# Softmax sums in another order: other merged pairs of P tiles, a later sum, and a new start of the output projection

## The chip, the cores and the metric

The kernel runs on one core of a Trainium2 chip. The metric is the device time of one execution in microseconds (us). TensorE (PE) multiplies matrices, VectorE (DVE), ScalarE (ACT) and GpSimd (POOL) do the elementwise work, and SyncE (SP) issues most DMAs.

## The reference

Two layers alternate over x of 2048 tokens by 1024 features, float32. `_A` is full softmax attention with 32 heads of 32 features; `_B` scores every token and passes only the eight best through a feed-forward block.

```python
def _A_ref(x, wqkv, wo):
    qkv = (x @ wqkv).reshape(B, S, 3, H, Dh).transpose(2, 0, 3, 1, 4)
    q, k, v = qkv[0], qkv[1], qkv[2]
    p = softmax(einsum("bhqd,bhkd->bhqk", q, k) * Dh ** -0.5)
    o = einsum("bhqk,bhkd->bhqd", p, v)
    return o.transpose(0, 2, 1, 3).reshape(B, S, D) @ wo

def _B_ref(x, w_r, w_gate, w_up, w_down):
    r = x @ w_r
    idx = argsort(-r)[:, :8]
    x_sel = take_along_axis(x, idx)
    y = ((silu(x_sel @ w_gate) * (x_sel @ w_up)) @ w_down) * sigmoid(r_sel)
    return x + scatter_add(zeros, idx, y)

for _ in range(2):
    x = x + _A_ref(layernorm(x), wqkv, wo)
    x = x + _B_ref(layernorm(x), w_r, w_gate, w_up, w_down)
```

## The kernel before

`layer(n, ...)` runs twice. Every engine works through its own list in the order in which the code writes it; what overlaps follows from semaphores alone.

**Projections of q, k and v** (`proj`). 24 column blocks (b) of the weights are multiplied with each of four chunks (c) of 512 tokens. Weights are float32 cut into two parts: ACT casts the high part `wh` from the loaded `wraw` (L498), POOL subtracts for the low part `wl` (L499), and a product is three matmuls, `wh` with `xh`, `wl` with `xh`, `wh` with `xl` (L552 to L554). Results go to DRAM, from where the attention's q and k are loaded. In the last chunk, at b = 3, SP issues the loads of the first keys, and from b = 6 on `proj` slips the first row maxima of the scores in between (`pre_half`, matmuls L444, maxima L448), which need the keys' first slot. That slot holds the high and low parts (j = 0 and 1) of a head; j = 2 fills the second slot. ACT's cast of each block's result is L567.

**Attention.** 32 units (eight groups of four heads, four chunks of 512 queries) of 16 steps each. A step takes 128 keys (kt) for four heads: PE computes scores (L459), ACT exponentiates them into one of nine `P` tiles (L758), and in the next step PE multiplies P with v (L684). Row maxima for a unit 25 steps ahead are found beside it, four reductions on DVE per step (L452) of scores that PE makes for it alone (L444). A new P tile overwrites the one of nine steps earlier, so its exponent waits for the last reader of that one.

The softmax denominators need the sum of all 16 P tiles of a unit. Two of them (`DIRECT`, 14 and 15) are summed by PE straight away. Five pairs are merged by an accumulating DMA that POOL issues (`MERGED`: tile k + 1 added into tile k, L697, 1 MB each), and POOL adds what is left, eight adds a unit, into `acc` (`ADDED`, pairs of a step and a tile, L694). At step `SUM_AT`, counted from the unit's start and so lying in the next unit, PE sums `acc` and the direct tiles with a matrix of ones (`sum_mm`, L704). These lists set the order on POOL:

```python
ev = [(k + 2, "end", 0, "merge", (k, k + 1)) for k in MERGED]
ev += [(at, "end", 1, "add", (k, 0 if at == ADDED[0][0] else None, False)) for at, k in ADDED]
return ev + [(SUM_AT, "mid", 5, "sum", ())]
```

The last unit of a layer does its adds on DVE, and its steps carry no more maxima.

**Output projection.** For each of 16 tiles of 128 tokens the attention's result `oraw` is scaled by the reciprocal denominators `rden` (L807), cut into `oh` (ACT, L810) and `ol` (DVE, L811), and multiplied with `woh` and `wol`, the two parts of `wo`, in 48 matmuls into one of two `pre` tiles (L850 to L854). DVE adds the residual x (L856), takes the layernorm (L120, L869) and the router's score (L870, which also writes into the `pre` tile and so frees it). The last unit's result and sums go to DRAM, and the second half of the denominators (`xn` from `sd`) is read back and inverted on DVE (L729) before the loop over tiles starts. In the second layer POOL scatters each finished tile to the output (L875). The feed-forward block follows; in the first layer it runs beside the next layer's projections.

## Time and profile before

| | before |
|---|---|
| median of three runs | 4854.77 us (4845.85 to 4872.93) |
| the profiled execution | 4860.6 us, of which the span of the instructions is 4858.7 us |
| busy: PE, DVE, POOL, ACT | 95%, 67%, 66%, 50% of the span |
| mean granted TensorE clock | 0.976 |

All durations below are from the one profiled execution. PE is busy nearly all the time, but a matmul's end is modelled, and a busy share over the whole span hides which stage waits for what. The two attentions take up the larger part of the span: the exponents run from 614.0 to 4525.9 us, with the output projection, the feed-forward block and the second projections between the layers.

### The profile page before, as it was taken

Reading aid. Unit: us, or ns where it says so; the run is one execution under the profiler, and the core shown is the slowest. Engines: PE = TensorE matmul, PEld = TensorE weight load, DVE = VectorE, ACT = ScalarE, POOL = GpSimd, SP = SyncE. Lnnn points to the kernel's source line nnn. Section 1 sums busy time; section 2 is a strip of 40 time slices with the busy share of each in tenths; the row PEclk is TensorE's granted clock in tenths of the full one; section 3 lists DMA queues with packets and bytes.
Section 4 is the critical chain, followed back from the end, with each engine's and each line's share of the span. In section 5 each row is a group of like instructions: output and inputs, shape, how many; then the busy total and the mean of one; then the engine's idle time right before and its main releaser. Section 6 shows DMA issues by size and latency. Waiting matters only on the chain. (4 is left out here: it accounts for less than half of the span.)

```text
span 4858.7 us, 73884 instructions
## 1 busy us (share of the span) xinstructions
PE 4609.1 (95%) x29438; PEld 2702.2 (56%) x29438; DVE 3233.4 (67%) x4943; ACT 2422.7 (50%) x2550; POOL 3227.5 (66%) x1251
## 2 busy tenths in 40 slices
PE   8999999999999999979799999999999999999796
PEld 6887745444444454437577777544444444444472
DVE  3221578788888888866522225888888888886753
ACT  2222266666666666640122222766676666767200
POOL 4443368888888888944433432888888888888341
PEclk9999999999999999999899999999999999999897
DMA  6656467676777777749688664867777777767477
GB/s 196 186 174 176 134 152 162 145 167 141 172 146 157 158 154 154 164 103 257 216 241 266 195 178 126 172 143 163 155 163 154 156 152 159 169 143 161 130 226 295
DMA packets 341433, 833.10 MB, mean 171 GB/s; under 512 B 43296, under 2 KB 175392, under 8 KB 291152
## 3 DMA queue, kind: packets, MB, share of 16 engines
q0 software_dynamic: 47168, 333.63, 34.1%
q1 hardware_dynamic: 284512, 465.38, 32.9%
q10 hardware_dynamic: 9408, 29.37, 2.3%
q8 instruction: 231, 3.78, 0.3%
q14 instruction: 114, 0.93, 0.1%
HBM read 384.01 MB, written 119.18 MB: 104 GB/s over the span
## 5 line engine op out<-in xcount | busy, mean ns | idle before, releaser
L452 DVE TENSOR_REDUCE nm<-st 128x1 f32<-128x512 f32 x3896 | 2424.6, 684 | 443.2 <-PE st L444 431.6
L758 ACT ACTIVATE P<-pre 128x1024 f32<-128x1024 f32 x2048 | 1985.7, 1022 | 771.9 <-PE pre L459 459.5
L694 POOL TENSOR_TENSOR acc<-acc,P 128x2048 f32<-128x2048 f32 x434 | 1999.2, 4607 | 406.1 <-DMA P<-P 346.0
L459 PE MATMUL pre<-q,ks 64*128 64x512 f32 (+1 forms) x8192 | 1162.0, 400 | 8.3 <-ACT P L758 7.5
L684 PE MATMUL pv<-P,v 128*32 128x512 f32 x8192 | 1094.8, 607 | 3.0 <-DMA v<-vd 3.0
L444 PEld LDWEIGHTS st<-ks,q 64*128 64x128 f32 x3896 | 536.1, 185 | 911.3 <-DVE nm L452 766.1
L444 PE MATMUL st<-ks,q 64*128 64x512 f32 x3896 | 973.6, 471 | 0.4
L499 POOL TENSOR_TENSOR wl<-wraw,wh 128x2048 fp32r<-128x2048 f32 (+1 forms) x97 | 441.9, 4556 | 683.4 <-ACT wh L498 651.3
L459 PEld LDWEIGHTS pre<-q,ks 64*128 64x128 f32 (+1 forms) x8192 | 774.3, 188 | 211.3 <-ACT P L758 79.7
L552 PE MATMUL st<-xh,wh 128*128 128x512 f32 x1536 | 617.0, 402 | 2.2 <-ACT xh L525 2.2
L554 PE MATMUL st<-xl,wh 128*128 128x512 f32 x1536 | 601.9, 392 | 0.6 <-DVE xl L526 0.5
L553 PE MATMUL st<-xh,wl 128*128 128x512 f32 x1536 | 600.7, 391 | 0.0
L568 DVE TENSOR_TENSOR lo<-st,hi 128x512 fp32r<-128x512 f32 x128 | 88.2, 689 | 434.0 <-ACT hi L567 434.0
L567 ACT CAST hi<-st 128x512 fp32r<-128x512 f32 x128 | 75.3, 588 | 566.3 <-PE st L554 566.3
L552 PEld LDWEIGHTS st<-xh,wh 128*128 128x128 f32 x1536 | 289.9, 189 | 107.1 <-issue 33.4
L697 POOL DMA_DIRECT2D P<-P x310 | 294.0, 948 | 64.7 <-PE st L444 64.1
L554 PEld LDWEIGHTS st<-xl,wh 128*128 128x128 f32 x1536 | 289.5, 188 | 64.5 <-DVE xl L526 1.7
L553 PEld LDWEIGHTS st<-xh,wl 128*128 128x128 f32 x1536 | 290.1, 189 | 56.1
L684 PEld LDWEIGHTS pv<-P,v 128*32 128x32 f32 x8192 | 162.2, 108 | 267.9 <-issue 263.1
L694 POOL TENSOR_TENSOR acc<-P 128x2048 f32<-128x2048 f32 x62 | 301.9, 4869 | 0.0
L850 PE MATMUL pre<-woh,oh 128*128 128x512 f32 x512 | 208.4, 407 | 53.1 <-DVE pre L870 43.1
L535 DVE COPY vn<-st 128x512 f32<-128x512 f32 x64 | 44.3, 691 | 304.0 <-PE st L533 304.0
(163 smaller groups left out, 2555.5 us busy)
## 6 DMA issues: line engine op xcount, KB each, us to landing
P<-P POOLq DMA_DIRECT2D x310, 1024.0 KB, 8.5
wraw<-in_A_wqkv_dram SPq DMA_DIRECT2D x96, 1024.0 KB
q<-qh SPq DMA_DIRECT2D x256, 128.0 KB
ks<-kh SPq DMA_DIRECT2D x128, 256.0 KB
fw<-in_B_w_down_dram SPq DMA_DIRECT2D x28, 1024.0 KB
qh<-hi SPq DMA_DIRECT2D x64, 256.0 KB
ql<-lo SPq DMA_DIRECT2D x64, 256.0 KB
kh<-hi SPq DMA_DIRECT2D x64, 256.0 KB
```

What stands on the lines that cost most here:

```text
L444: pe.matmul(ps[b], Q[u][rows, i, 0, qt * 128:(qt + 1) * 128], KS[(u // QC) % 2][rows, i, 0, j * 512:(j + 1) * 512], start=True, stop=True, ...
L452: dve.tensor_reduce(NM[u][:, j, 2 * i + b:2 * i + b + 1, qt], ps[b], axis=AX.X, op=OP.max, negate=True)
L459: pe.matmul(p[:, b * 512:(b + 1) * 512], KS[(u // QC) % 2][rows, i, slot, kt * 128:(kt + 1) * 128], Q[u][rows, i, slot, :], start=(slot == ...
L499: pool.tensor_tensor(wl[:, :, sl], raw[:, :, sl], wh[:, :, sl].bitcast(F32), op=OP.subtract)
L552: pe.matmul(p, wh[:, a, wsl], xh[:, a, :], start=(a == 0), stop=False)
L553: pe.matmul(p, wl[:, a, wsl], xh[:, a, :], start=False, stop=False)
L554: pe.matmul(p, wh[:, a, wsl], xl[:, a, :], start=False, stop=(a == KD - 1))
L684: pe.matmul(PV[u][32 * h:32 * h + 32, :], V[g][:, kt, 32 * h:32 * h + 32], P[s][:, h, :], start=(kt == 0), stop=(kt == NT - 1), tile_posit ...
L694: (dve if on_dve else pool).tensor_tensor(o, a, P[u * NT + k].rearrange("p h c -> p (h c)"), op=OP.add)
L697: pool.dma_start(P[u * NT + a], P[u * NT + b], accum_op=OP.add)
L758: act.activation(P[s][:, 2 * i:2 * i + 2, :].rearrange("p h c -> p (h c)"), p, AF.Exp, scale=SCALE)
L850: pe.matmul(p[:, bl], oh[:, a, :], woh[:, a, bl], start=(a == 0), stop=False)
```

## The change

Four edits. The pairs to merge are now written with their step, `(2, 0)` merging tiles 0 and 1 at step 2; pairs, order and steps of POOL's adds are others, and the sum is one step later. In the projections the first maxima start at b = 7, and the keys are loaded j by j, so that the first slot of all heads comes first. At the start of the output projection all eight casts `woh` are ACT's and all eight subtractions `wol` are DVE's, alternating; the loads stand in another order, and both `oraw` tiles are scaled first. In the loop over tiles the reciprocal of the second half stands behind the first tile's residual add and the third tile's split, and PE's matmuls go block by block of `wo`, both halves of the output in each.

```diff
-MERGED = (2, 4, 6, 8, 11)
-ADDED = ((5, 1), (7, 2), (8, 4), (12, 6), (13, 8), (14, 10), (17, 11), (19, 13))
+MERGED = ((2, 0), (8, 6), (11, 8), (13, 10), (15, 12))
+ADDED = ((5, 3), (6, 0), (9, 5), (12, 4), (14, 6), (15, 8), (16, 10), (20, 12))
+FIRST = 2
-SUM_AT = 21
+SUM_AT = 22
-    ev = [(k + 2, "end", 0, "merge", (k, k + 1)) for k in MERGED]
-    ev += [(at, "end", 1, "add", (k, 0 if at == ADDED[0][0] else None, False)) for at, k in ADDED]
+    ev = [(at, "end", 0, "merge", (k, k + 1)) for at, k in MERGED]
+    ev += [(at, "end", 1, "add", (k, FIRST if at == ADDED[0][0] else None, False)) for at, k in ADDED]
...
-                proj(2 * wb + i, c, c == 3 and b >= 6)
+                proj(2 * wb + i, c, c == 3 and b >= 7)
...
-                        for h in range(4):
-                            for j in range(3):
+                        for j in range(3):
+                            for h in range(4):
                                 load_k(0, h, j)
...
-            load_o(0, sync)
-            load_o(1, sync)
-            load_x(0)
-            split_o(0)
             woh = wp.tile([128, KD, D], F32R, name="woh", bufs=1)
+            load_x(0)
+            wrb = wp.tile([128, D], F32, name="wrb", bufs=1)
+            load_o(0, sync)
+            load_o(1, sync)
+            for t in range(2):
+                scale_o(t)
+                OT[t] = tuple(wp.tile([128, NG, 128], F32R, name=i) for i in ("oh", "ol"))
...
-            for a in range(KD):
-                (act.copy, dve.tensor_copy)[a % 2](woh[:, a, :], WOR[:, a, :])
-            for a in range(KD):
-                (dve, pool)[a % 2].tensor_tensor(wol[:, a, :], WOR[:, a, :], woh[:, a, :].bitcast(F32), op=OP.subtract)
+            for a in range(KD):
+                act.copy(woh[:, a, :], WOR[:, a, :])
+                if a == 0:
+                    split_o(0)
+                dve.tensor_tensor(wol[:, a, :], WOR[:, a, :], woh[:, a, :].bitcast(F32), op=OP.subtract)
             split_o(1)
+            load_x(1)
             load_o(2)
             load_o(3)
+            dma(wrb, w_r[None, :].to_broadcast([128, D]))
...
             sum_load(second, 1)
-            recip(second, 1)
-            dma(wrb, w_r[None, :].to_broadcast([128, D]))
...
                 if t + 2 < NT:
                     split_o(t + 2)
+                if t == 0:
+                    recip(second, 1)
```

On POOL, in the attention's first unit before the change: the tiles of steps 2 to 10 are 4194, 4224, 4254, 4285, 4317, 4349, 4389, 4421 and 4451, those of 11 to 13 are 4482, 4512 and 4542; the last two rows belong to the next unit.

```order
L694 TENSOR_TENSOR acc_4314<-acc_4314,P_4194 128x2048
L697 DMA P_4317<-P_4349 128x2048
L694 TENSOR_TENSOR acc_4314<-acc_4314,P_4254 128x2048
L697 DMA P_4389<-P_4421 128x2048
L694 TENSOR_TENSOR acc_4314<-acc_4314,P_4317 128x2048
L697 DMA P_4482<-P_4512 128x2048
L694 TENSOR_TENSOR acc_4314<-acc_4314,P_4389 128x2048
L694 TENSOR_TENSOR acc_4314<-acc_4314,P_4451 128x2048
L694 TENSOR_TENSOR acc_4314<-acc_4314,P_4482 128x2048
L694 TENSOR_TENSOR acc_4314<-acc_4314,P_4542 128x2048
L697 DMA P_4697<-P_4727 128x2048
L694 TENSOR_TENSOR acc_4837<-P_4632,P_4665 128x2048
```

The same place after the change; here steps 4 to 13 are 4255, 4285, 4317, 4349, 4388, 4419, 4450, 4480, 4511 and 4541, and the next unit begins with 4632.

```order
L698 DMA P_4317<-P_4349 128x2048
L695 TENSOR_TENSOR acc_4314<-acc_4314,P_4285 128x2048
L698 DMA P_4388<-P_4419 128x2048
L695 TENSOR_TENSOR acc_4314<-acc_4314,P_4255 128x2048
L698 DMA P_4450<-P_4480 128x2048
L695 TENSOR_TENSOR acc_4314<-acc_4314,P_4317 128x2048
L698 DMA P_4511<-P_4541 128x2048
L695 TENSOR_TENSOR acc_4314<-acc_4314,P_4388 128x2048
L695 TENSOR_TENSOR acc_4314<-acc_4314,P_4450 128x2048
L698 DMA P_4632<-P_4666 128x2048
L695 TENSOR_TENSOR acc_4314<-acc_4314,P_4511 128x2048
L695 TENSOR_TENSOR acc_4818<-P_4697,P_4728 128x2048
```

Before, one add stands between the merge into 4317 and the add that reads it, and likewise for 4389; now two adds stand between each merge and its add.

On DVE, at the start of the first layer's output projection, before:

```order
L811 TENSOR_TENSOR ol<-oraw,oh 128x1024
L827 CAST woh<-wor 128x1024 x4
L829 TENSOR_TENSOR wol<-wor,woh 128x1024 x4
L807 TENSOR_TENSOR oraw<-oraw,rden 128x1024
L811 TENSOR_TENSOR ol<-oraw,oh 128x1024
L729 RECIPROCAL xn<-xn 64x512
L856 TENSOR_TENSOR x<-pre,x 128x1024
L807 TENSOR_TENSOR oraw<-oraw,rden 128x1024
L811 TENSOR_TENSOR ol<-oraw,oh 128x1024
L120 BN_STATS bst<-x 128x6 x2
```

And after:

```order
L807 TENSOR_TENSOR oraw<-oraw,rden 128x1024 x2
L816 TENSOR_TENSOR ol<-oraw,oh 128x1024
L836 TENSOR_TENSOR wol<-wor,woh 128x1024 x8
L816 TENSOR_TENSOR ol<-oraw,oh 128x1024
L863 TENSOR_TENSOR x<-pre,x 128x1024
L807 TENSOR_TENSOR oraw<-oraw,rden 128x1024
L816 TENSOR_TENSOR ol<-oraw,oh 128x1024
L730 RECIPROCAL xn<-xn 64x512
L121 BN_STATS bst<-x 128x6 x2
```

The four casts are gone from DVE, four subtractions are added, and the reciprocal has moved behind three operations of the first and third tile.

On SP, the loads of the first keys in the first layer's last chunk, after the change (before, the twelve `ks` rows go head by head, `kh`, `kl`, `kh` for each):

```order
L72 DMA ks0_126<-kh0_109 32x2048 x4
L72 DMA ks0_126<-kl0_110 32x2048 x4
L72 DMA ks0_126<-kh0_109 32x2048 x4
L72 DMA wraw_3213<-in_A_wqkv_dram 128x8x256
L72 DMA qh0_107<-hi_3240 128x512
```

The twelve loads are the same and the weight block `wraw_3213`, used from b = 8 on, still stands directly behind them; the eight of the first slot now come first, where the last of them was the eleventh.

## Rows read from the trace of the kernel before

**Rows 1.** Groups of instructions over the whole span: busy us, mean ns, idle before.

```profile
L452 DVE TENSOR_REDUCE nm<-st 128x1 f32<-128x512 f32 x3896 | 2424.6, 684 | 443.2 <-PE st L444 431.6
L694 POOL TENSOR_TENSOR acc<-acc,P 128x2048 f32<-128x2048 f32 x434 | 1999.2, 4607 | 406.1 <-DMA P<-P 346.0 <-PE st L444 24.8 <-PE pre L459 12.4
L758 ACT ACTIVATE P<-pre 128x1024 f32<-128x1024 f32 x2048 | 1985.7, 1022 | 771.9 <-PE pre L459 459.5 <-ACT P L758 156.9 <-POOL acc L694 115.8
...
L694 POOL TENSOR_TENSOR acc<-P 128x2048 f32<-128x2048 f32 x62 | 301.9, 4869 | 0.0
L697 POOL DMA_DIRECT2D P<-P x310 | 294.0, 948 | 64.7 <-PE st L444 64.1 <-ACT P L758 0.6
```

**Rows 2.** One line's instructions in three stretches (one copy a unit): count, first and last start.

```profile
L709 ACT COPY o<-pv x30: 591/592/593, 663.7 to 2048.0; 128x512 f32<-128x512 f32 x30
...
L709 ACT COPY o<-pv x30: 590/592/593, 3071.4 to 4441.7; 128x512 f32<-128x512 f32 x30
...
L709 ACT COPY o<-pv x5: 590/592/592, 3071.4 to 3254.7; 128x512 f32<-128x512 f32 x5
```

**Rows 3.** Timeline of DVE in one step: start, duration, [idle before <-who ended it].

```profile
1226.71 2.48 DVE L452 TENSOR_REDUCE nm<-st 128x1 f32<-128x512 f32 x4 [0.22 <-PE st L444]
```

**Rows 4.** Timeline of POOL within one unit.

```profile
1217.61 0.88 POOL L697 DMA_DIRECT2D P<-P  x1
1222.09 4.58 POOL L694 TENSOR_TENSOR acc<-acc,P 128x2048 f32<-128x2048 f32 x1 [3.60 <-DMA P<-P]
1226.62 0.87 POOL L697 DMA_DIRECT2D P<-P  x1
...
1231.94 1.01 POOL L697 DMA_DIRECT2D P<-P  x1
```

**Rows 5.** DMA issues of the page: count, KB each, median us to landing.

```profile
P<-P POOLq DMA_DIRECT2D x310, 1024.0 KB, 8.5
```

**Rows 6.** Adds (L694) in the second layer's last unit: stretch, DVE busy, POOL busy.

```profile
4485.40:4503.30 17.90, 17.58 (x3) 15.56 (x3) 0.88 0.06 16
4503.30:4527.60 24.30, 22.92 (x10) 0.00 (x0) 0.95 0.05 14
```

**Rows 7.** Timeline of ACT around b = 6 of the first layer's last chunk.

```profile
476.00 0.59 ACT L567 CAST hi<-st 128x512 fp32r<-128x512 f32 x1 [4.85 <-PE st L554]
492.28 1.91 ACT L498 CAST wh<-wraw 128x2048 fp32r<-128x2048 f32 x1 [15.69 <-DMA wraw<-in_A_wqkv_dram]
495.72 0.59 ACT L567 CAST hi<-st 128x512 fp32r<-128x512 f32 x1 [1.53 <-PE st L554]
502.95 0.59 ACT L567 CAST hi<-st 128x512 fp32r<-128x512 f32 x1 [6.64 <-PE st L554]
```

**Rows 8.** Timeline of POOL at the same place.

```profile
494.27 4.60 POOL L499 TENSOR_TENSOR wl<-wraw,wh 128x2048 fp32r<-128x2048 f32 x1 [22.06 <-ACT wh L498]
```

**Rows 9.** Stretch: PE, PEld, DVE, ACT, POOL busy, granted clock, DMA share, GB/s.

```profile
482.00:492.00 10.00, 4.29 (x9) 2.83 (x10) 1.87 (x2) 0.00 (x0) 0.00 (x0) 0.51 1.05 245
```

**Rows 10.** Timeline of DVE at the start of the second layer's output projection.

```profile
4531.90 1.23 DVE L807 TENSOR_TENSOR oraw<-oraw,rden 128x1024 f32<-128x1024 f32 x1 [4.32 <-DMA rden<-rd]
...
4542.15 9.00 DVE L829 TENSOR_TENSOR wol<-wor,woh 128x1024 fp32r<-128x1024 f32 x4
...
4553.40 1.23 DVE L811 TENSOR_TENSOR ol<-oraw,oh 128x1024 fp32r<-128x1024 f32 x1 [1.12 <-ACT oh L810]
4567.17 3.34 DVE L729 RECIPROCAL xn<-xn 64x512 f32<-64x512 f32 x1 [12.54 <-DMA xn<-sd]
...
4575.03 1.28 DVE L120 BATCH_NORM_STATS2 bst<-x 128x6 f32<-128x512 f32 x2
```

**Rows 11.** Timeline of PE: the third tile's first matmul there.

```profile
4579.78 0.77 PE L850 MATMUL pre<-woh,oh 128*128 128x512 f32 x1 [13.96 <-DVE pre L870]
```

**Rows 12.** One line's instructions, both layers: duration ns min/median/max.

```profile
L829 DVE TENSOR_TENSOR wol<-wor,woh x8: 1212/2304/3408, 2147.7 to 4549.9; 128x1024 fp32r<-128x1024 f32 x8
```

**Rows 13.** Timeline of SP at the start of the first layer's output projection.

```profile
2133.13 1.71 SPq L803 DMA_DIRECT2D rden<-rd  x4
```

More of the change, by code (lines that the diff above doesn't have):

```diff
@@ L803, in load_o, with scale_o @@
                     eng.dma_start(RD[t][32 * h:32 * h + 32], rd[t, h:h + 1].to_broadcast([32, NG, 128]))
+            def scale_o(t):
+                dve.tensor_tensor(OR[t], OR[t], RD.pop(t), op=OP.mult)
             def split_o(t):
+                if t not in OT:
+                    scale_o(t)
+                    OT[t] = tuple(wp.tile([128, NG, 128], F32R, name=i) for i in ("oh", "ol"))
                 raw = OR.pop(t)
-                dve.tensor_tensor(raw, raw, RD.pop(t), op=OP.mult)
-                oh = wp.tile([128, NG, 128], F32R, name="oh")
-                ol = wp.tile([128, NG, 128], F32R, name="ol")
+                oh, ol = OT[t]
                 act.copy(oh, raw)
                 dve.tensor_tensor(ol, raw, oh.bitcast(F32), op=OP.subtract)
-                OT[t] = (oh, ol)
             def load_x(t):
@@ L835, in layer @@
             store_sum(NU - 1, last_sum, rest[:, 512:1024])
-            second = wp.tile([128, D], F32, name="xn", bufs=1)[0:64, 0:512]
+            second = XN[0:64, 0:512]
             sum_load(second, 1)
-            recip(second, 1)
-            dma(wrb, w_r[None, :].to_broadcast([128, D]))
             wor.close()
@@ L847, in layer @@
                 halves = [slice(0, 512), slice(512, 1024)]
-                for bl in halves:
-                    for a in range(KD):
+                for a in range(KD):
+                    for bl in halves:
                         pe.matmul(p[:, bl], oh[:, a, :], woh[:, a, bl], start=(a == 0), stop=False)
                         pe.matmul(p[:, bl], ol[:, a, :], woh[:, a, bl], start=False, stop=False)
-                for bl in halves:
-                    for a in range(KD):
+                for a in range(KD):
+                    for bl in halves:
                         pe.matmul(p[:, bl], oh[:, a, :], wol[:, a, bl], start=False, stop=(a == KD - 1))
```

8 lines of the change are left out of this document (5 added, 3 removed).

## Prediction

> **What bounds the kernel now.** I read the groups by line first, because PE's busy share hides who waits for whom. The reader should look at the idle columns. POOL's add waits 346.0 us for the merging DMA, ACT's exponent 115.8 us for POOL's add, and the maxima on DVE 431.6 us for the scores [rows 1]. One chain joins them: a merge lands late, POOL's add stands, a P buffer is released late, the exponent and then the scores of that step come late.
>
> So is POOL the pace-maker of a unit? Both layers together have 62 units whose adds are POOL's. Per unit POOL is busy (1999.2 + 301.9) / 62 = 37.1 us with adds and 294.0 / 62 = 4.7 us with issuing merges, and stands 346.0 / 62 = 5.6 us for them [rows 1]: 47.4 us. The units follow each other at (2048.0 - 663.7) / 29 = 47.73 us in the first layer and (4441.7 - 3071.4) / 29 = 47.25 us in the second [rows 2]. POOL has no slack, so yes. What would the pace be without it? The second layer's first four periods, before POOL falls behind, take 183.3 / 4 = 45.83 us [rows 2]. That fits DVE: its four maxima of a step take 2.48 us plus 0.22 us of waiting [rows 3], and 16 x 2.70 = 43.2 us, with 2.6 us left for what happens once in a unit.
>
> The timeline of POOL shows the wait itself. The merge issued at 1226.62 is needed after one add and one more issue, at 1232.95; the add begins at 1237.64, 11.0 us after the issue, and has stood 4.69 us [rows 4]. The median merge lands after 8.5 us [rows 5].
>
> **Attention: the main term.** Adds, merges and the work of DVE keep their number; the order changes. By the rows of the program two adds now stand between each merge and the add that reads it. From issue to use that is two issues of about 0.9 and two adds of 4.58 us, 11.0 us [rows 4], against 6.3 before. The median merge is hidden with 2.5 us to spare, the slow one of the timeline just so. POOL's unit falls to 37.1 + 4.7 = 41.8 us, 4.0 below the 45.83 of DVE, and this slack takes up the occasional later merge. DVE then sets the pace: 29 x (47.73 - 45.83) = 55.1 us in the first layer, 29 x (47.25 - 45.83) = 41.2 us in the second, **96 us**. Bounds: nothing, if merges get as much slower as they get more time; not more than 96, since DVE's steps are untouched. I take the full amount, because the four undisturbed periods are a measurement of exactly that state. The later sum costs nothing as long as `acc` and the direct tiles are there; what it could lose is a P buffer held a step longer, which the 4 us cover.
>
> The Trainium skill, page "DMA: Bandwidth & Descriptors", section "Issuing engines are not separate DMA queues", says that transfers issued by different engines run on the same 16 engines and interleave. Both rows agree that a merge has no fixed time (8.5 us in the median, 11.0 us in that unit); by the rule the new steps could meet other loads and run longer, which is the first rival below (4767), and by the rows the sum stays as it is.
>
> **Last unit of a layer.** There DVE adds. While POOL still has adds left, three DVE adds take 17.90 us, 5.97 each; afterwards ten take 24.30 us, 2.43 each [rows 6]. With POOL no longer late, I take one of its three remaining adds as done before: 3.5 us a layer, **7 us**, bounds 0 and 7.
>
> **Projections, b = 6 to 8.** Block 6 lasts from 476.00 to 495.72, 19.7 us, block 7 7.2 us [rows 7]; the excess of 12.5 us is the wait for the keys' first slot, and TensorE's granted clock falls to 0.51 (the 1.2 GHz level) in it, with the DMA engines full [rows 9]. After the change the first maxima start a block later and the first slot lands earlier, so this wait goes. What is late next? The weight block behind the same twelve loads: the same bytes stand in front of it, so it still lands at about 492.28; the cast ends at 494.2 and POOL's subtraction runs from 494.27 to 498.87 [rows 7, 8]. Block 8, which began at about 502.9, can begin at 498.9 at best: 4.0 us. In the idle time that now lies ahead of block 8 the clock may fall again, for which I take off 1.5 us. For the second layer, which I take as equal, the same: **5 us**. Bounds: 0, and 2 x 12.5 = 25 if the weight block comes sooner.
>
> **Start of the output projection.** On DVE the chain from the first scaling to the end of the second `ol` takes from 4531.90 to 4554.63, 22.7 us [rows 10], four subtractions beside POOL's four taking 9.00 of it; where POOL is idle one takes 1.21 us, elsewhere up to 3.41 [rows 12]. Afterwards two scalings, `ol`, eight subtractions and `ol` are twelve operations at 1.21 us, 14.5 us: 8.2 saved. ACT's eight casts run one ahead of the subtractions; were each 1 us longer, all 8.2 would be gone, which is the lower bound. The reciprocal starts 12.54 us after the second `ol` [rows 10], since it waits for a store, a sum and a load that stand behind it, and this distance stays. Before, the residual add, the scaling and `ol` of the third tile stood behind it, from its end at 4570.51 to 4575.03; now they lie inside the wait: 4.5 saved. The third tile's matmuls start 4.75 us behind that point, after 13.96 us of waiting for its `pre` tile [rows 10, 11], and I let both savings arrive there: 12.7 us a layer.
>
> The loads differ by layer. In the second the chain begins after 4.32 us of idle for `rden` [rows 10], whose loads now wait only for the last unit's early adds; this idle goes, 17 us in all. In the first, SP issued the four `rden` loads at 2133.13, 0.43 us each [rows 13]; x and the second `oraw` now stand ahead and the second scaling waits for five more loads, so I take off 3 us (estimate from five to nine issues of 0.43): 9.7. Together **27 us**; bounds 9 (only the reciprocal's 4.5 twice) and 34 (17 twice). From there on the tiles follow as before, so I carry the saving to the end. The new order of PE's matmuls has the same number of them: nothing.
>
> **Sum.** 96 + 7 + 5 + 27 = 135 us. The profiled execution took 4860.6 us, so 4725.6; it lies 5.8 us above the median of the runs, against which that is **4719 us**.
>
> **Rivals.**
> 1. *Merges slow down where they now stand, and half of the attention's gain is lost.* Speaks for it: the 11.0 us of [rows 4] just fill the new distance. Against: 8.5 us in the median, and 4 us of slack per unit. It needs some 5 us of waiting a unit, as much as now. Time: 4719 + 48 = 4767. Chance 0.12.
> 2. *The start of the output projection gains nothing*, because the reciprocal's load is late by as much as the chain is shorter. For: the 12.54 us are a chain of DMAs. Against: it starts from the end of that chain. Time: 4719 + 27 = 4746. Chance 0.11.
> 3. *Slower: a merge is read too late to free its P buffer.* Tiles 4 and 6 are now added only at steps 12 and 14, one step before the exponents nine tiles on reuse them. If POOL stood there for two merges of 4.69 us beyond the new distance in every unit, a unit would take 41.8 + 9.4 = 51.2 us, against a mean of 47.5 now: 58 x 3.7 = 215 us lost, 4719 + 96 + 215 = 5030. It decides from 47.5 + 39 / 58 = 48.2 us a unit. Against: that takes merges of over 15 us. Chance 0.03.
> 4. *The keys' edit does all it can*, with the weight block landing early: 4719 - 20 = 4699. Against: the same twelve loads stand ahead of it. Chance 0.06.
>
> **How the numbers follow.** My forecast has 0.68. The range runs from 4690 (rival 4, with the upper bound of the output projection, 7 us, taken in) to 4765, just short of rival 1; it contains rival 2, and what falls outside is most of rival 1, rival 3 and some error in the rest, together under 0.2. By itself the likeliest case spans 4700 to 4740. A measurement of this kernel can tell about 0.5% from no change, 24 us, so 4830 to 4879 counts as the same. All cases but rival 3 and a loss of nearly the whole attention term lie below: faster 0.94, the same 0.03, slower 0.03.
>
> **What would show it.** POOL's add waits for the merging DMA drop from 346 us to under 100, the exponents' wait for POOL's add to near nothing, and the copies once a unit follow at 45.8 us: right for attention. If POOL still waits and the period stays above 46.6 us, rival 1 holds. Block 6 lasts about as long as a block without a wait, and the idle time stands ahead of block 8, ended by the weights' subtraction: right for the keys. On DVE the twelve operations take 14.5 us, the reciprocal starts 12.5 us after them and the third tile starts 17 and 10 us sooner after the last unit's end: right for the output projection. The prediction is wrong if DVE's step gets longer with POOL's new rhythm, for then the 45.83 us don't hold.

## The result and the profile after

The changed kernel took 4723.81 us in the median of four runs (4714.38 to 4733.07), the kernel before 4850.94 us in four runs: a ratio of 0.9729 (95% interval 0.9692 to 0.9767). The medians differ by 127.1 us. The profiled execution has a span of 4726.1 us, 132.6 us less than before, and a mean granted clock of 0.983.

The groups by line (busy us, mean ns, idle before) answer to [rows 1]:

```profile
L453 DVE TENSOR_REDUCE nm<-st 128x1 f32<-128x512 f32 x3896 | 2418.5, 683 | 343.0 <-PE st L445 337.2
L695 POOL TENSOR_TENSOR acc<-acc,P 128x2048 f32<-128x2048 f32 x434 | 2103.2, 4846 | 78.7 <-DMA P<-P 68.7 <-PE st L445 2.4
L759 ACT ACTIVATE P<-pre 128x1024 f32<-128x1024 f32 x2048 | 1986.1, 1022 | 722.4 <-PE pre L460 523.7 <-ACT P L759 179.6 <-POOL acc L695 14.7
```

The three idle columns have moved together: POOL's add waits 68.7 us for merges (346.0 before), the exponents 14.7 us for POOL's add (115.8 before), and the maxima 337.2 us for scores (431.6 before). The copy of a unit's result answers to [rows 2]; the columns are the minimum, median and maximum duration, and the first and the last start:

```profile
L710 ACT COPY o<-pv x30: 593/594/596, 663.0 to 1992.3; 128x512 f32<-128x512 f32 x30
...
L710 ACT COPY o<-pv x30: 593/594/597, 3000.7 to 4329.1; 128x512 f32<-128x512 f32 x30
```

(1992.3 - 663.0) / 29 = 45.84 us in the first layer and (4329.1 - 3000.7) / 29 = 45.81 us in the second, where 45.83 had been forecast. POOL within one unit of the first layer (start, duration, idle before), which answers to [rows 4]:

```profile
1124.17 0.88 POOL L698 DMA_DIRECT2D P<-P  x1 [0.46 <-PE st L445]
...
1142.94 0.88 POOL L698 DMA_DIRECT2D P<-P  x1 [4.06 <-PE st L445]
1143.56 4.88 POOL L695 TENSOR_TENSOR acc<-acc,P 128x2048 f32<-128x2048 f32 x1
1148.35 0.94 POOL L698 DMA_DIRECT2D P<-P  x1
1148.96 4.93 POOL L695 TENSOR_TENSOR acc<-acc,P 128x2048 f32<-128x2048 f32 x1
1153.76 0.98 POOL L698 DMA_DIRECT2D P<-P  x1
1154.38 4.99 POOL L695 TENSOR_TENSOR acc<-acc,P 128x2048 f32<-128x2048 f32 x1
```

The page's row of the merges (count, KB each, median us to landing) answers to [rows 5]:

```profile
P<-P POOLq DMA_DIRECT2D x310, 1024.0 KB, 8.8
```

In this unit no add waits for a merge. POOL waits ahead of two merges, until the tiles to merge are free (the view names PE's matmuls as what ends it): 0.46 and 4.06 us. Over the first layer's 29 periods it stands some 4.7 us a unit, 3.3 of them ahead of merges and 1.2 for merges to land; the prediction had given it 4.0 us of slack. The mean of an add has risen from 4607 to 4846 ns, but POOL hardly works slower: behind a merge's issue the record of the add begins before that of the issue ends (1142.94 + 0.88 lies after 1143.56). Counted without this overlap, POOL is busy 41.1 us of a unit, and 40.9 before. From one issue to the next, an issue and an add take 1148.35 - 1142.94 = 5.41 us.

Which engine sets the 45.8 us now? The first layer's 29 periods in the changed kernel (busy us of PE, PEld, DVE, ACT, POOL, then granted clock, DMA share, GB/s), and DVE's maxima of two steps:

```profile
663.00:1992.30 1329.30, 1328.51 (x9978) 670.84 (x9978) 1163.23 (x1915) 930.87 (x988) 1192.53 (x378) 1.00 0.75 164
```

```profile
1226.45 2.48 DVE L453 TENSOR_REDUCE nm<-st 128x1 f32<-128x512 f32 x4 [0.22 <-PE st L445]
...
1231.72 2.48 DVE L453 TENSOR_REDUCE nm<-st 128x1 f32<-128x512 f32 x4 [2.49 <-PE st L445]
```

DVE is busy 1163.23 / 29 = 40.1 us of a unit. It stands 0.22 us a step for PE's scores, and once a unit, beside PE's sum, 2.49 us. PE shows no gap worth naming (1328.51 of 1329.30 us), though the ends of its matmuls are modelled; in turn its weight loads for these scores wait 364.7 us in these periods for DVE's maxima. DVE and PE thus wait for each other in nearly every step. That DVE alone sets the pace, as the prediction has it, is not shown; no kernel here makes the work of either shorter.

Where the 132.6 us lie, measured in the two traces between the same events:

| stretch | before | after | gain |
|---|---|---|---|
| start to the first exponent | 614.0 | 613.2 | 0.8 |
| exponents of the first layer | 1520.5 | 1459.9 | 60.7 |
| last exponent to the last tile's matmuls, first layer | 199.3 | 188.7 | 10.6 |
| from there to the second layer's first exponent | 692.0 | 693.4 | -1.4 |
| exponents of the second layer | 1501.1 | 1454.7 | 46.4 |
| last exponent to the last tile's matmuls, second layer | 213.2 | 194.8 | 18.4 |
| from there to the end | 118.6 | 121.5 | -2.9 |

### The profile page after: what moved, and what is told of

It reads as the page before. It is cut to its first block, busy times and chain, and to the rows that moved or that the text cites. A ratio compares the mean times of both kernels' runs of the same rounds, so it can differ in the third digit from the quotient of the medians.

```text
span 4726.1 us, 73912 instructions
## 1 busy us (share of the span) xinstructions
PE 4570.0 (97%) x29438; PEld 2708.1 (57%) x29438; DVE 3211.9 (68%) x4943; ACT 2429.3 (51%) x2558; POOL 3217.7 (68%) x1243
## 4 chain that ended last, share of the span: by engine, by line
PE 88%; DMA 6%; DVE 3%; issue 2%; POOL 1%; ACT 0%; SPq 0%; ACTq 0%; POOLq 0%; DVEq 0%
PE pv L685 21%; PE pre L460 20%; PE st L445 15%; PE st L553 7%; PE st L555 7%; PE st L554 7%; PE st L705 3%; DMA out_dram<-x,pi 3%; PE pre L857 1%; PE pre L858 1%; PE pre L861 1%; PE pv L328 1%; DVE acc L695 1%; PE pre L445 1%; PE st L534 1%
## 5 line engine op out<-in xcount | busy, mean ns | idle before, releaser
L453 DVE TENSOR_REDUCE nm<-st 128x1 f32<-128x512 f32 x3896 | 2418.5, 683 | 343.0 <-PE st L445 337.2
L695 POOL TENSOR_TENSOR acc<-acc,P 128x2048 f32<-128x2048 f32 x434 | 2103.2, 4846 | 78.7 <-DMA P<-P 68.7
L460 PE MATMUL pre<-q,ks 64*128 64x512 f32 (+1 forms) x8192 | 1141.8, 396 | 4.2 <-ACT P L759 4.2
L857 PE MATMUL pre<-woh,oh 128*128 128x512 f32 x512 | 206.9, 404 | 27.5 <-DVE pre L879 22.7
```

Of the source, the lines that this page charges most:

```text
L453: dve.tensor_reduce(NM[u][:, j, 2 * i + b:2 * i + b + 1, qt], ps[b], axis=AX.X, op=OP.max, negate=True)
L460: pe.matmul(p[:, b * 512:(b + 1) * 512], KS[(u // QC) % 2][rows, i, slot, kt * 128:(kt + 1) * 128], Q[u][rows, i, slot, :], start=(slot == ...
L695: (dve if on_dve else pool).tensor_tensor(o, a, P[u * NT + k].rearrange("p h c -> p (h c)"), op=OP.add)
L857: pe.matmul(p[:, bl], oh[:, a, :], woh[:, a, bl], start=(a == 0), stop=False)
```

## The experiments

Beside the change twelve kernels were run. Ratios are to the kernel before on the same chip, and us are medians; the kernel before took 4851 to 4862 us on the chips used, so small differences are read from ratios and from stretches of the traces.

| kernel | us | ratio (95%) |
|---|---|---|
| the change | 4723.8 | 0.9729 (0.9692 to 0.9767) |
| attention's edit alone | 4747.4 | 0.9768 (0.9752 to 0.9784) |
| sum back at step 21 | 4727.4 | 0.9731 (0.9714 to 0.9747) |
| old order, sum at 22 | 4796.8 | 0.9877 (0.9849 to 0.9905) |
| old order, sum at 21 | 4844.0 | 0.9970 (0.9956 to 0.9983) |
| one add between | 4790.0 | 0.9858 (0.9842 to 0.9875) |
| four merges | 4763.1 | 0.9816 (0.9782 to 0.9849) |
| three merges | 4927.6 | 1.0136 (1.0103 to 1.0169) |
| keys undone | 4732.9 | 0.9736 (0.9707 to 0.9765) |
| weights before keys | 4713.6 | 0.9701 (0.9675 to 0.9726) |
| keys in two parts | 4703.4 | 0.9671 (0.9655 to 0.9686) |
| output start undone | 4742.2 | 0.9750 (0.9735 to 0.9765) |
| reciprocal before the loop | 4730.1 | 0.9719 (0.9702 to 0.9737) |

### Is it the attention, and is it the distance from merge to add?

**Attention's edit alone**: in the kernel before, `MERGED`, `ADDED`, `FIRST` and the sum's step are set as in the change, nothing else.

```diff
-MERGED = (2, 4, 6, 8, 11)
+MERGED = ((2, 0), (8, 6), (11, 8), (13, 10), (15, 12))
...
-SUM_AT = 21
+SUM_AT = 22
...
```

> The kernel before with only the new pairs, order and steps of the merges and adds and the sum at step 22. My theory, by which POOL no longer waits for merges, expects the whole attention part of the gain here: units of 45.8 us, the two stretches of exponents about 60 and 46 us shorter than before, so about 4745 us. A rival, that the attention's gain needs something of the other edits (loads that lie elsewhere), expects a unit mean above 46.5 us and more than 4780 us.

It took 4747.4 us. The two stretches of exponents are 1460.0 and 1455.1 us long, 60.5 and 46.0 less than before, and nearly as in the changed kernel. So the attention's gain needs nothing of the other edits, and it is most of the whole.

**One add between**: only the steps of three merges are later, so that a single add stands between them and the add that reads them.

```diff
-MERGED = ((2, 0), (8, 6), (11, 8), (13, 10), (15, 12))
+MERGED = ((2, 0), (11, 6), (13, 8), (15, 10), (15, 12))
```

> The changed kernel with three of the five merges issued later (into tile 6 at step 11, 8 at 13, 10 at 15), so that one add instead of two stands between each and the add that reads it. Pairs, adds, their order and the sum stay. By the distance theory each of the three waits 2 to 3 us: POOL's unit becomes 41.8 + 6 to 9 = 48 to 51 us, the unit mean rises over 45.8 to the same, and the time is 4724 + 58 x (2 to 5) = 4840 to 5010 us. If other pairs or an earlier release of P buffers made the gain, the time stays at about 4724 us.

It took 4790.0 us, 66 us more than the change. The groups by line of this kernel:

```profile
L695 POOL TENSOR_TENSOR acc<-acc,P 128x2048 f32<-128x2048 f32 x434 | 2039.5, 4699 | 359.1 <-DMA P<-P 251.7 <-PE st L445 39.1 <-PE pre L460 38.7
L759 ACT ACTIVATE P<-pre 128x1024 f32<-128x1024 f32 x2048 | 1985.3, 1022 | 778.6 <-PE pre L460 554.2 <-DMA P<-P 101.6 <-ACT P L759 61.3
```

The wait for merges is back, 251.7 us or 4.1 us a unit, with the same pairs and the same adds in the same order. All that stands ahead of the adds is 359.1 us, 5.8 a unit; with 41.0 us of work that is 46.8 us, and the copies once a unit follow at 46.8. POOL's own list thus accounts for the loss, and the distance is a cause. It is not the only thing that the edit moves: the exponents wait for merges now too (101.6 us), since the second tile of a pair is freed only when its later merge has landed, and no kernel separates the two. The loss is below the 116 us that I had set as its least: the three merges together waited 4.1 us a unit instead of 6 to 9, and a part of that falls into POOL's slack.

### What is the later sum worth?

**Sum back at step 21**: one number of the changed kernel.

```diff
-SUM_AT = 22
+SUM_AT = 21
```

> The changed kernel with the sum at step 21 as before, and the merges and adds of the change. The last add stands at the end of step 20 and takes 4.85 us, nearly two steps, so PE would stand some 2 to 3 us for it in its own order in every unit. If the later sum is a needed part of the edit: 58 x 2 = about 115 us slower than the changed kernel, 4840 us. If the sum's step is without weight, as my sum had it: 4724 us, within 10.

4727.4 us: no difference, and my 115 us did not come. I had put the last add at the step where the code writes it. But POOL is not bound to steps; it does its list as soon as the semaphores let it. In the changed kernel the add written at step 20 starts in step 18 of its unit's count, so the sum at 21 finds it done. The sum's matmuls wait 9.3 us for POOL over the whole kernel, 0.15 us a unit.

**Old order, sum at 22**, and **old order, sum at 21**: the changed kernel with the pairs, steps and order of before, and in the second also with the sum as before.

```diff
-MERGED = ((2, 0), (8, 6), (11, 8), (13, 10), (15, 12))
-ADDED = ((5, 3), (6, 0), (9, 5), (12, 4), (14, 6), (15, 8), (16, 10), (20, 12))
+MERGED = (2, 4, 6, 8, 11)
+ADDED = ((5, 1), (7, 2), (8, 4), (12, 6), (13, 8), (14, 10), (17, 11), (19, 13))
...
```

> The changed kernel with the pairs, order and steps of the merges and adds of before, but the sum at step 22. If the distance from merge to add is the cause of the gain, POOL's waits come back (about 5 us a unit) and the time is about 4724 + 107 = 4830 us. The rival is that the sum came too early before, so that PE stood for the last add; then this kernel keeps the gain, 4724 to 4745 us.

> The changed kernel with pairs, steps and order of merges and adds and the sum's step all as before. With the old order and the sum at step 22 the time was 0.9877 of before, with the new order and the sum at 21 it was 0.9731, as good as the changed kernel's 0.9729. If the two parts interact (the late adds of the old order make PE stand for acc in the sum, the new order's do not), this kernel loses the whole attention term, 107 us: about 4830 us, and the sum on PE waits some 70 us for POOL's add again. If the parts simply add up, it is 0.9877 + 0.0002 of before, about 4797 us.

The first took 4796.8 us, the second 4844.0. So the four combinations do not add up: moving the sum by a step is worth 47 us with the old order (0.9970 to 0.9877) and nothing with the new one (0.9731 to 0.9729). The first matmuls of the sum that read `acc`, by line, in the kernel with the old order and the sum at 22, and below in the one with the sum at 21:

```profile
L704 PE MATMUL st<-acc,ones 128*32 128x512 f32 x512 | 66.7, 593 | 3.5 <-DVE acc L694 2.4 <-POOL acc L694 1.1
```

```profile
L704 PE MATMUL st<-acc,ones 128*32 128x512 f32 x512 | 73.6, 649 | 77.6 <-POOL acc L694 77.6
```

With POOL late, the sum at step 21 stops PE for 77.6 us in all (70.5 in the kernel before, 2.3 after the change), and with it the scores of the following steps; one step later it does not. What remains of the loss at step 22, 4796.8 - 4723.8 = 73 us, is POOL's own pace: the stretches of exponents are 1491.2 and 1492.4 us long, 69.0 more than in the change. In the first layer POOL is busy 41.0 us of a unit there and stands 5.9, 5.0 of them for merges, and 46.9 us is what a unit takes.

### How much slack has POOL?

**Four merges** and **three merges**: pairs (0, 1) and then also (6, 7) are not merged; POOL adds these tiles one by one, with nine and ten adds a unit.

```diff
-MERGED = ((2, 0), (8, 6), (11, 8), (13, 10), (15, 12))
-ADDED = ((5, 3), (6, 0), (9, 5), (12, 4), (14, 6), (15, 8), (16, 10), (20, 12))
+MERGED = ((8, 6), (11, 8), (13, 10), (15, 12))
+ADDED = ((4, 1), (6, 2), (7, 3), (9, 5), (12, 4), (14, 6), (15, 8), (16, 10), (20, 12))
```

```diff
+MERGED = ((11, 8), (13, 10), (15, 12))
+ADDED = ((4, 1), (6, 2), (7, 3), (9, 5), (11, 4), (13, 6), (14, 7), (15, 8), (16, 10), (20, 12))
```

> The changed kernel with four merges instead of five: tiles 0 and 1 are added by POOL (nine adds a unit; the merges into 6, 8, 10 and 12 stay where they are). This prices POOL's slack. The prediction gave POOL 41.8 us of work in a unit of 45.83; an add more and a merge's issue less make 41.8 + 4.6 - 0.95 = 45.5 us, just inside. By that budget the time stays within 15 us of the changed kernel, 4724 to 4739 us. A rival, that POOL's slack is already used up by the 68.7 us of waits left and by longer adds (4.85 us in mean in the changed kernel's groups), expects about 47 us a unit, 58 x 1.2 = 70 us slower.

> The changed kernel with three merges (into 8, 10 and 12) and ten adds a unit. POOL's work is 41.8 + 2 x 3.65 = 49.1 us, 3.3 above DVE's 45.8: if POOL sets the pace as soon as its work exceeds DVE's, 58 x 3.3 = 190 us slower than the changed kernel, about 4915 us. If the pace is set by something else than POOL's own list (PE's sums, the release of P buffers), it comes out under 4800 us.

Three merges: 4927.6 us, 204 us more than the change, slower than before; 190 were expected. In the first layer the units follow each other every 48.75 us, and POOL hardly stands at all:

```profile
L695 POOL TENSOR_TENSOR acc<-acc,P 128x2048 f32<-128x2048 f32 x558 | 2638.5, 4728 | 32.2 <-ACT P L759 2.4 <-DMA P<-P 1.0
L759 ACT ACTIVATE P<-pre 128x1024 f32<-128x1024 f32 x2048 | 1981.5, 1022 | 929.1 <-PE pre L460 487.7 <-POOL acc L695 280.0 <-DMA P<-P 68.1
```

The add waits 1.0 us for merges, and the exponents 280.0 us for POOL's add. That settles that POOL sets the pace as soon as its own list is longer than the 45.8 us that a unit takes otherwise. By the pitch of the records, 5.41 us for an issue with an add and 4.66 for an add that follows an add (1111.84 to 1116.50 in this kernel's timeline), the list is 3 x 5.41 + 7 x 4.66 = 48.9 us long here, within 0.1 us of the 48.75, and 5 x 5.41 + 3 x 4.66 = 41.0 us in the change. With four merges it is 4 x 5.41 + 5 x 4.66 = 44.9 us, still inside a unit, but the time was 4763.1 us, 39 us more, between my two expectations. The groups show both of POOL's waits, for merges 81.9 us (1.3 a unit) and, ahead of a unit's first add, for exponents 47.2 us; 44.9 + 1.3 = 46.2 us, and the trace has 46.15 us a unit:

```profile
L695 POOL TENSOR_TENSOR acc<-acc,P 128x2048 f32<-128x2048 f32 x496 | 2406.4, 4852 | 99.0 <-DMA P<-P 81.9 <-ACT P L759 1.5 <-DMA q<-qh 0.7
L695 POOL TENSOR_TENSOR acc<-P 128x2048 f32<-128x2048 f32 x62 | 284.2, 4584 | 47.2 <-ACT P L759 47.2
```

So a slack of 0.9 us did not cover the waits: here merges land after 10.2 us in the median, and their landing varies by several microseconds.

### The keys

In the changed kernel, block 7 of the first layer's last chunk takes from 481.58 to 498.79 us, 17.2 instead of 7.2. The timelines of ACT, DVE and PE there (they answer to [rows 7] to [rows 9]):

```profile
491.09 1.90 ACT L499 CAST wh<-wraw 128x2048 fp32r<-128x2048 f32 x1 [14.16 <-DMA wraw<-in_A_wqkv_dram]
493.00 0.58 ACT L568 CAST hi<-st 128x512 fp32r<-128x512 f32 x1
```

```profile
493.62 0.69 DVE L569 TENSOR_TENSOR lo<-st,hi 128x512 fp32r<-128x512 f32 x1 [15.97 <-ACT hi L568]
494.23 4.61 DVE L449 TENSOR_REDUCE nm<-pre 128x2 f32<-128x1024 f32 x4
```

```profile
483.03 0.74 PE L445 MATMUL pre<-ks,q 64*128 64x512 f32 x4
...
495.50 0.79 PE L445 MATMUL pre<-ks,q 64*128 64x512 f32 x2 [8.10 <-DVE nm L449]
```

Read upwards from PE: the maxima's matmuls at 483.03 no longer wait for keys. The next ones, at 495.50, wait 8.10 us for DVE to empty their PSUM tile. DVE's maxima stand behind the low part of block 6, this behind ACT's cast of block 6, and this behind ACT's cast of the weight block, which waits 14.16 us for a DMA. The late weight block stops PE through three in-order queues, one block before the weights are needed. It is late because SP issues it only at 480.26, 11 us behind the first key load, for a reason given at the end.

**Keys undone**: keys head by head and maxima from b = 6, as before, in the changed kernel.

```diff
-                proj(2 * wb + i, c, c == 3 and b >= 7)
+                proj(2 * wb + i, c, c == 3 and b >= 6)
...
-                        for j in range(3):
-                            for h in range(4):
+                        for h in range(4):
+                            for j in range(3):
```

> The changed kernel with the keys as before: loaded head by head, and the first maxima from b = 6. I forecast 5 us for this edit; the traces show that the exponents of the first layer begin only 0.8 us sooner than before, and that the second layer loses 0.9 us from its last chunk to its first exponent. So I now expect no difference, 4724 us within what is measurable; by the forecast it would be 4729 us, which the stretch from block 3 to the first exponent in the trace tells apart.

4732.9 us, ratio 0.9736: not to be told from the change by its time. From block 3 to the first exponent it takes 155.1 us in the first layer and 154.9 in the second; the change takes 153.4 and 155.8. By these two traces the edit is worth 1.7 us in one layer and costs 0.9 in the other. More can be read from the other kernels, since nine have this part of the code as changed and three as before: with the code of before the stretch takes 154.5 to 155.1 us in all six places, with the changed code 151.1 to 155.8, in the median 153.4 in the first layer and 153.8 in the second. So the edit is worth some 1.5 and 1.1 us.

**Weights before keys**: the weight block ahead of the twelve loads, the four loads of the second slot at b = 6.

```diff
-                    if k + 4 < len(steps):
+                    if k + 4 < len(steps) and (c, b) != (3, 4):
...
                     if b == 3:
+                        load_w(steps[k + 5][1])
-                        for j in range(3):
+                        for j in range(2):
                             for h in range(4):
                                 load_k(0, h, j)
+                    if b == 6:
+                        for h in range(4):
+                            load_k(0, h, 2)
```

> The changed kernel, but in the last chunk the weight block for b = 8 is issued before the twelve key loads instead of behind them, and the four loads of the keys' second slot go out at b = 6. In the changed kernel ACT's cast of that block waits 14.2 us for it, the cast of the result of block 6 stands behind it on ACT, DVE's low part and maxima behind that, and PE stops for 8 to 9 us inside block 7. If the late weight block is the cause, the stop and the slow clock behind it go: 11 us in the first layer and 13 in the second, less up to 4.3 us each if the keys' first slot is then late; 4700 to 4712 us. If the DMA engines are the bound there, whatever the order, PE waits for the keys as long as now and the time stays at 4724 us.

4713.6 us; block 3 to the first exponent takes 149.0 and 150.3 us, 4.4 and 5.5 less than in the change. Nearly half of what the next kernel gains is gained here. In what is left of the stop, block 7 still takes 14.2 us, and the timeline of PE there names other transfers:

```profile
486.29 0.47 PE L445 MATMUL pre<-ks,q 64*128 64x512 f32 x1 [2.56 <-DMA qh<-hi]
487.18 2.10 PE L445 MATMUL pre<-ks,q 64*128 64x512 f32 x3 [0.42 <-DMA ks<-kl]
```

**Keys in two parts**: tokens 0 to 1535 are loaded in the third chunk, where they are ready, and the weight block goes ahead of the rest.

```diff
-        def load_k(g, h, i):
+        def load_k(g, h, i, sl=slice(0, S)):
...
-                    if k + 4 < len(steps):
+                    if k + 4 < len(steps) and (c, b) != (3, 4):
...
+                if c == 2 and b in (14, 16, 18):
+                    for h in range(4):
+                        load_k(0, h, (b - 14) // 2, slice(0, 1536))
                 if c == 3:
...
                     if b == 3:
+                        load_w(steps[k + 5][1])
                         for j in range(3):
                             for h in range(4):
-                                load_k(0, h, j)
+                                load_k(0, h, j, slice(1536, S))
```

> The changed kernel with the first keys loaded in two parts: tokens 0 to 1535 in the third chunk (at b = 14, 16 and 18, slot by slot), when they are ready, and only tokens 1536 to 2047 at b = 3 of the last chunk, with the weight block for b = 8 issued ahead of them. With the weight block ahead of whole key loads block 7 still took 14.2 and 15.4 us, 7 to 8 over its 7.2. If the 3 MB of keys in one piece are the cause of what is left, no block of the last chunk exceeds 7.7 us and the granted clock stays at full speed there: 11 + 13 = 24 us faster than the changed kernel, 4700 us. If PE's stop has another cause, it stays as in the kernel with the weights ahead, 4714 us.

4703.4 us, ratio 0.9671 (0.9655 to 0.9686), about 20 us less than the change by the medians and the fastest kernel here. Block 3 to the first exponent takes 143.7 and 142.5 us, 9.7 and 13.3 less than in the change. Three stretches of this kernel, and below of the change (busy us of PE, PEld, DVE, ACT, POOL, then granted clock, DMA share, GB/s):

```profile
470.00:482.00 12.00, 12.00 (x55) 9.93 (x54) 1.38 (x2) 3.09 (x3) 3.50 (x2) 1.00 0.79 188
482.00:498.00 16.00, 14.57 (x65) 9.81 (x64) 9.68 (x10) 3.49 (x4) 7.13 (x2) 1.00 0.98 258
498.00:510.00 12.00, 12.00 (x55) 8.37 (x54) 9.05 (x9) 2.57 (x3) 3.46 (x2) 1.00 0.39 131
```

```profile
470.00:482.00 12.00, 12.00 (x54) 9.95 (x53) 1.38 (x2) 1.17 (x2) 2.54 (x1) 1.00 1.05 253
482.00:498.00 16.00, 7.57 (x30) 4.86 (x29) 4.38 (x5) 2.48 (x2) 4.51 (x1) 0.80 0.99 279
498.00:510.00 12.00, 12.00 (x47) 8.09 (x46) 7.40 (x8) 2.97 (x3) 4.59 (x1) 0.84 0.53 154
```

PE hardly stops any more, and its clock stays at the 2.4 GHz level where it fell to a mean of 0.80 before. Block 7 takes 9.0 us in the first layer (not under 7.7, as expected) and 7.6 in the second. With most of the keys out of the burst of loads the stop is nearly gone, so the burst was its cause. What the order within it is worth alone is not shown: the kernel with the weights ahead gains 4.4 and 5.5 us, but it also takes four of the twelve loads out of the burst.

### The start of the output projection

**Output start undone**: loads, scaling, split of `wo` and reciprocal as before; the rest as changed.

```diff
             for a in range(KD):
-                act.copy(woh[:, a, :], WOR[:, a, :])
...
+                (act.copy, dve.tensor_copy)[a % 2](woh[:, a, :], WOR[:, a, :])
+            for a in range(KD):
+                (dve, pool)[a % 2].tensor_tensor(wol[:, a, :], WOR[:, a, :], woh[:, a, :].bitcast(F32), op=OP.subtract)
```

> The changed kernel with the start of the output projection as before: loads, scaling, split of wo among ACT, DVE and POOL, and the reciprocal before the loop. By my steps and by the traces (last tile 10.6 us sooner after the last exponent in the first layer, 18.4 in the second, 3 lost at the end) it is 26 us slower than the changed kernel, 4750 us. By rival 2, that this start gains nothing, 4724 us.

**Reciprocal before the loop**: only the reciprocal moves back.

```diff
             sum_load(second, 1)
+            recip(second, 1)
...
-                if t == 0:
-                    recip(second, 1)
```

> The changed kernel with only the reciprocal of the second half moved back ahead of the loop over tiles, and so ahead of the first residual add and the third tile's scaling and split on DVE. By my step these 4.5 us lie behind the reciprocal again, and the third tile's matmuls start 4.5 us later in both layers: 4724 + 9 = 4733 us. In the second layer the third tile waits only 3.47 us in the changed kernel, so 8 us there would show it. If something else releases the third tile, its start does not move.

The first took 4742.2 us (4750 by my steps), the second 4730.1 (4733). Their ratios, 0.9750 and 0.9719, have intervals that overlap with the change's, so the traces have to decide. DVE in the changed kernel, at the start of the second layer's output projection, answers to [rows 10]:

```profile
4413.82 1.22 DVE L807 TENSOR_TENSOR oraw<-oraw,rden 128x1024 f32<-128x1024 f32 x1
4415.73 1.23 DVE L807 TENSOR_TENSOR oraw<-oraw,rden 128x1024 f32<-128x1024 f32 x1 [0.68 <-DMA rden<-rd]
...
4418.00 9.17 DVE L836 TENSOR_TENSOR wol<-wor,woh 128x1024 fp32r<-128x1024 f32 x8
4427.09 1.22 DVE L816 TENSOR_TENSOR ol<-oraw,oh 128x1024 fp32r<-128x1024 f32 x1
...
4438.01 3.35 DVE L730 RECIPROCAL xn<-xn 64x512 f32<-64x512 f32 x1 [1.49 <-DMA xn<-sd]
```

The chain takes 4428.31 - 4413.82 = 14.5 us, as worked out (22.7 before), and the reciprocal has only 1.49 us of waiting ahead of it, since the three operations now lie there. The third tile's first matmul, in the changed kernel, with the reciprocal ahead of the loop, and with the whole start undone (each on the time axis of its own trace):

```profile
4446.07 0.47 PE L857 MATMUL pre<-woh,oh 128*128 128x512 f32 x1 [3.47 <-DVE pre L879]
```

```profile
4451.14 0.77 PE L858 MATMUL pre<-woh,oh 128*128 128x512 f32 x1 [9.51 <-DVE pre L878]
```

```profile
4469.42 0.76 PE L851 MATMUL pre<-woh,oh 128*128 128x512 f32 x1 [13.30 <-DVE pre L871]
```

PE's wait is 3.47, 9.51 and 13.30 us. From the last exponent to this matmul it is 36.2 us in the change, 41.9 with the reciprocal ahead and 52.2 with the start undone; in the first layer 44.6, 45.9 and 51.0. So by these traces the reciprocal's place is worth 5.7 us in the second layer, but only 1.3 of the expected 4.5 in the first, and the whole start 16.0 and 6.4 us.

These differences hold more than the edit. From the reciprocal's end to the third tile it is 4.7 us in both layers of all ten kernels that have this start as changed, and 9.27 us in the four that have the reciprocal ahead of the loop: its place is worth 4.5 us, as worked out. But the time from the second `ol` to the reciprocal, a chain of DMAs, did not stay at 12.5 us; it is 9.7 to 14.2 us in the ten kernels. In the first layer of the changed kernel it is 13.5 us, against 10.3 with the reciprocal ahead, which takes back 3.2 of the 4.5. There the second scaling, too, waits for its loads within the chain:

```profile
2083.51 1.23 DVE L807 TENSOR_TENSOR oraw<-oraw,rden 128x1024 f32<-128x1024 f32 x1 [2.93 <-DMA rden<-rd]
...
2109.58 3.34 DVE L730 RECIPROCAL xn<-xn 64x512 f32<-64x512 f32 x1 [6.44 <-DMA xn<-sd]
```

To the last tile's matmuls the whole start is worth only 204.2 - 194.8 = 9.4 us in the second layer; in the first it is 8.1. The chain of waits of the changed kernel, traced back from its end, says why the second layer loses (start, duration, what the time went to):

```profile
4418.09 9.08 DVE wol L836 x8
4458.89 10.66 DMA out_dram<-x,pi
4470.33 11.25 DMA out_dram<-x,pi
...
4575.74 12.93 DMA out_dram<-x,pi
4601.19 3.63 PE pre L861 x16
```

From 4458.89 on, ten scatters of finished tiles follow each other on POOL, one every 11.0 to 14.5 us, while PE needs 10.9 us for a tile. What the start gains ahead of them is partly waited out again. The first layer has no scatters.

## Why the prediction was right, and where it was off

The time came out 5 us above the forecast, inside its narrow range, and no rival held. The main term has its size right, and its mechanism but for the engine that sets the new pace. Of the three smaller ones the last units came near by luck, the output projection gave 17 us of 27 and the keys 2.6 of 5, read over all kernels; with these the terms add up to 97 + 10 + 17 + 3 = 127 us, as the medians have it. By its terms:

- **Attention, 96 us: right.** The 29 periods of the two layers give 55.0 and 41.9 us. That POOL had no slack, and that the unit falls to 45.83 us without its waits, was right to 0.02 us, and the experiments show it from both sides: with the merges nearer to their adds POOL's waits return, and with more adds POOL is the bound again. That it is DVE which sets the 45.83 is not shown (above); the number holds all the same, since it was read from four undisturbed periods. The merges land after 8.8 us in the median (8.5 before) and 14.6 at most (13.8 before). So rival 1's slower merges hardly came, and neither did the longer run that the interleaving rule of the Trainium skill, "DMA: Bandwidth & Descriptors", section "Issuing engines are not separate DMA queues", had left possible; in the order chosen here the trace decides for the rows.
- **Last units, 7 us: 10.2, by another way.** They are 5.7 and 4.5 us shorter. But no slow add of DVE has gone: three still run beside POOL's adds, as before. What has gone is PE's stop in the sum of the unit before, which falls into this one: 7.0 and 5.5 us before, 1.1 in both layers now. That the size was near is luck.
- **One part of the mechanism was missing.** The prediction put the whole loss down to POOL's list. With the old order, 47 us of it come through PE, which stopped in the sum at step 21 for an `acc` that POOL finished late. It cured itself with POOL's delay, so the sum of the prediction did not suffer; a kernel with only the later sum would have been forecast wrongly, as it was in my expectation for it.
- **Keys, 5 us: mis-sized.** By the two traces it is nothing, by all kernels some 2.6 us. Block 8 of the first layer starts 4.0 us earlier, as worked out. But the maxima that block 6 no longer does are only moved: a block with maxima takes 7.23 us and one without 5.44, so 1.8 us come back in blocks 18 and 19, and the slow clock takes 1.3 (block 8 lasts 8.57 us in place of 7.23, with a granted clock of 0.84 in its stretch). The prediction had taken off 1.5 for the clock and nothing for the moved work. Also, PE's idle time did not lie ahead of block 8, ended by POOL's subtraction; it lay inside block 7, ended by DVE, behind ACT's cast.
- **Output projection, 27 us: DVE's own work right, the loads and the carry to the end wrong.** The twelve operations and the reciprocal's place came as worked out. The prediction let the distance from the second `ol` to the reciprocal stay, and counted the 4.32 us of idle for `rden` as saved. In the second layer the third tile starts 16.6 us sooner than before: 1.0 because the chain starts sooner (DVE's last adds now end 4.0 us after the last exponent, so the idle time was mostly filled, not saved), 8.2 from the chain, 2.8 because the reciprocal's load came sooner, and 4.5 from the reciprocal's place. That this lies near the 17 forecast is luck. In the first layer it is 6.5 us (9.7 forecast): the chain starts 3.4 us later (3 taken off), is 6.0 shorter instead of 8.2, and the reciprocal's load comes 0.7 later. "I carry the saving to the end" failed in the second layer: of 16.0 us that this edit gives at the third tile, 9.4 arrive at the last. In the first, 8.1 arrive. Behind the last tiles 1.2 and 1.7 us are lost, and the spans differ by 15.1 us in all.

The traces of before and after differ by 29.0 us in the two stretches from the last exponent to the last tile's matmuls, but that is no proof of the 27: with the attention's edit alone and this code as before, the last tiles already lie 1.9 and 6.4 us nearer to the last exponent. Ten kernels have this code as changed, and in them the stretch takes 186.6 to 191.7 us in the first layer and 190.1 to 206.0 in the second, so 6.4 us lie within the spread. By the medians of these ten and of the three kernels with the code as before, the edit gives 7.7 and 9.5 us at the last tile, 17 in all.

The sum, 135 us, stands against 132.6 in the traces: the attention with the last units gave 4.1 us more, the two stretches of the output projection 2.0 more, the keys 5.1 less, and 3.4 us are lost behind the last tiles of the two layers.

## What to carry to other kernels

An in-order engine that uses the result of a DMA should have as much other work between the issue and the use as the DMA takes, with room for the slow ones; count that distance in the engine's own list, not in the steps of the loop, since an engine runs ahead of the step where its work is written. Compare the length of each engine's list in a unit with the pace of the unit: here a slack of 4 to 5 us hid nearly all waits, 0.9 us did not, and where the list was longer than the pace, it became the new pace to 0.1 us. Before reordering loads that arrive late, look whether part of them can go out earlier: the new order of the key loads, with the maxima a block later, gave 1 to 2 us a layer; less data in the burst, with the weights ahead, gave 10 to 13 more.

## What the runs showed of the hardware

- A merge of 1 MB from SBUF to SBUF has no steady duration: the median is 8.0 us with three merges a unit, 10.2 with four, 8.8 with five in the new order and 9.9 in the kernel with one add between, where two are issued back to back.
- Late loads can be the program's doing and not a queue's. In the changed kernel the first four key loads are issued in 1.97 us and the next four in 4.89 us, so the weight block's load goes out at 480.26, 11 us after the first of them:

```profile
469.32 1.97 SPq L72 DMA_DIRECT2D ks<-kh  x4
471.33 4.89 SPq L72 DMA_DIRECT2D ks<-kl  x4
...
480.26 0.40 SPq L72 DMA_DIRECT2D wraw<-in_A_wqkv_dram  x1
```

  SP waits there for earlier transfers to land, as its waits from 466 to 482 us show (us in total, times, longest). Eight semaphores go round among its DMAs in this stretch, and each one issued waits for the one eight before it: the third `kl` load for a store of `kh` issued at 468.44, the weight block for the first `kl` load.

```profile
SPq L72 <- DMA kh<-hi: 2.2, 1, 2.2
SPq L72 <- DMA ks<-kh: 1.9, 3, 0.7
```

- In the last unit of both layers of the changed kernel, the second and third DVE add, which run beside POOL's adds, take 6.45 to 6.49 us, the first, which begins within one of POOL's, 3.83 and 3.84, and the ten behind POOL's last add 2.29 us each. The long ones are the slow adds of [rows 6].
